# Whole-batch DMA transposes of queries and zero-padded keys in an attention and convolution kernel on one core

## The chip, the cores and the metric

One core of one Trainium2 chip. The metric is device time in microseconds (us) of one execution; medians of several executions are quoted. The kernel before takes 475.0 us (median of 3 runs, 474.39 to 475.42).

## The reference, cut to what matters

```python
B, H, S, D = 8, 12, 448, 64
scores = q @ k.transpose(0, 1, 3, 2) / sqrt(64)          # per batch and head, 448 x 448
attn   = exp(scores - m) / (sum(exp(scores - m)) + exp(-m))
x      = (attn @ v) -> (8, 448, 768)
proj   = x @ w_proj                                       # 768 -> 3 x 768
x1, x2, x3 = thirds of proj
y      = x1 * irfft(rfft(x2) * rfft(filter)) * x3         # along the 448 positions
out    = y @ w_out
```

## The kernel before

The kernel's matmuls contract over the partitions, so queries and keys must lie with the 64 head dimensions on partitions, while memory has positions there. The kernel works in pairs of heads (6 per batch, 48 in all). GpSimd's DMA queue loads a batch with the cast from float32 to bfloat16, and TensorE turns each pair: four key blocks and four query blocks, copied from PSUM by VectorE into a zero-padded key tile and a query tile.

```python
def transposes(A, hp):                       # one unit per pair, cut
    for t in range(4):                       # keys
        nc.tensor.transpose(tb[:, t*128:(t+1)*128], A["kn"][:, hp, t, :], ident_bf)
    for st in range(NST):                    # queries
        nc.tensor.transpose(tb[:, 512 + ...], A["qf"][:, st, hs, :], ident_bf[:SP, :SP])
    nc.vector.tensor_copy(z[0:64, 4:0:-1, :], tk[0:64])
    nc.vector.tensor_copy(z[64:128, 4:8, :], tk[64:128])
    nc.vector.tensor_copy(qT, tq)

# order of one pair's units ("cur" is scored, "old" is summed, "nxt" is turned)
sc(0); sc(1); av(0); T(nxt); sc(2); av(1); sc(3); back(old); folds(old)
```

Between these units the main loop puts dense units (projection, spectrum, gate, output) of the batch before, in a fixed ratio of listed costs. Each engine runs its instructions in program order: in the changed kernel below, TensorE does nothing for 44 us behind one waiting matmul. Batch 0 is loaded as float32 by SyncE's queue and cast by the engines.

The softmax here doesn't subtract the row's maximum and nothing guards it: scores larger than these inputs give would overflow.

## Time and profile before

| | before |
|---|---|
| time | 475.0 us |
| busy: TensorE, VectorE, ScalarE | 426.3, 307.3, 288.2 us of a span of 472.9 |
| TensorE busy from 200 to 250 us | 49.03 of 50 |
| one batch in steady state | 52.6 us |
| TensorE full from | 65.6 us |
| tail after TensorE's last attention unit (it starts at 429.63 us) | about 43 us, on TensorE dense work alone |

The prediction shows the main lines. VectorE's copies behind the transposes, from the groups by shape (line, engine, operation, out<-in, count | busy us, mean ns | idle before):

```profile
L338 DVE COPY kz<-tps 64x512 bf16<-64x512 bf16 x48 | 20.5, 428 | 0.7
L337 DVE COPY kz<-tps 64x512 bf16<-64x512 bf16 x48 | 19.7, 411 | 10.7 <-PE tps L329 10.7
L345 DVE COPY qT<-tps 128x448 bf16<-128x448 bf16 x42 | 16.4, 391 | 0.6
```

And what TensorE waits for from 66 to 420 us (who <- for whom: total us, times, longest), which is nearly nothing and lies in the spectrum units:

```profile
PE xsp L492 <- DVE g L519: 3.2, 7, 0.5
PE xsp L492 <- ACT x L517: 1.7, 7, 0.2
```

### The profile page before, as it was taken

Reading aid. Unit: us, or ns where it says so; the run is one execution under the profiler, and the core shown is the slowest. Engines: PE = TensorE matmul, PEld = TensorE weight load, DVE = VectorE, ACT = ScalarE, POOL = GpSimd, SP = SyncE. Lnnn points to the kernel's source line nnn. Section 1 sums busy time; section 2 is a strip of 40 time slices with the busy share of each in tenths; the row PEclk is TensorE's granted clock in tenths of the full one; section 3 lists DMA queues with packets and bytes.
Section 4 is the critical chain, followed back from the end, with each engine's and each line's share of the span. In section 5 each row is a group of like instructions: output and inputs, shape, how many; then the busy total and the mean of one; then the engine's idle time right before and its main releaser. Section 6 shows DMA issues by size and latency. Waiting matters only on the chain.

```text
span 472.9 us, 9624 instructions
## 1 busy us (share of the span) xinstructions
PE 426.3 (90%) x3872; PEld 298.9 (63%) x3872; DVE 307.3 (65%) x892; ACT 288.2 (61%) x493; POOL 109.4 (23%) x146
## 2 busy tenths in 40 slices
PE   0276889999999999999999999999999999999995
PEld 0144457577766777577766777577766777567664
DVE  7778555785569665774579575874578565873450
ACT  1364557666675667566675657657676668563543
POOL 5816391061202610071103510081000000000000
PEclk9998889999999999999999999999999999999999
DMA  7999999099901993097902991096900110003003
GB/s 208 181 231 176 146 161 62 1 73 134 89 1 11 138 129 19 1 88 120 89 1 20 144 129 5 1 101 126 69 1 1 60 60 0 2 2 119 0 1 116
DMA packets 128492, 35.62 MB, mean 75 GB/s; under 512 B 116925, under 2 KB 124864, under 8 KB 128448
## 3 DMA queue, kind: packets, MB, share of 16 engines
q0 software_dynamic: 118080, 19.87, 55.8%
q1 hardware_dynamic: 10368, 15.14, 10.9%
q8 instruction: 30, 0.49, 0.4%
q14 instruction: 14, 0.11, 0.1%
HBM read 43.86 MB, written 11.01 MB: 116 GB/s over the span
## 4 chain that ended last, share of the span: by engine, by line
PE 67%; DVE 14%; ACT 7%; DMA 7%; POOL 3%; issue 1%; SPq 1%; ACTq 0%; DVEq 0%; POOLq 0%
PE pps L508 18%; PE pps L473 10%; PE ops L580 10%; PE sc L353 9%; PE op L372 5%; DMA wproj_bf<-in_moe_w_proj_dram 4%; PE ops L558 3%; ACT xs L493 3%; PE cps L532 2%; PE xsp L492 2%; DVE t L496 2%; PE xps L395 2%; DVE g L519 2%; PE op L367 2%; DVE t L497 2%; ACT e L355 2%
## 5 line engine op out<-in xcount | busy, mean ns | idle before, releaser
L355 ACT ACTIVATE e<-sc 128x896 bf16<-128x896 f32 x144 | 132.6, 922 | 46.7 <-PE sc L353 46.7
L508 PE MATMUL pps<-xT,wproj_bf 128*128 128x448 bf16 x576 | 124.3, 352 | 0.5 <-ACT x L517 0.3
L508 PEld LDWEIGHTS <-wproj_bf 128*128 128x128 bf16 x576 | 53.5, 97 | 44.4 <-issue 3.0
L353 PE MATMUL sc<-qT,kz 128*128 128x448 bf16 x288 | 81.0, 364 | 0.5 <-ACT e L355 0.4
L473 PE MATMUL pps<-wproj_bf,xf 128*113 128x384 bf16 x384 | 72.2, 326 | 0.5 <-ACT x L480 0.5
L372 PE MATMUL op<-vn,e 128*128 128x65 bf16 x1152 | 58.1, 195 | 0.0
L473 PEld LDWEIGHTS <-xf 128*113 128x113 bf16 x384 | 48.9, 132 | 13.1 <-issue 0.9
L372 PEld LDWEIGHTS <-e 128*128 128x128 bf16 x1152 | 51.4, 98 | 6.8 <-issue 0.7
L580 PE MATMUL ops<-wout_bf,yT 128*112 128x384 bf16 x288 | 53.8, 327 | 0.5 <-ACT osb L568 0.5
L115 POOL DMA_DIRECT2D qf<-in_q_dram x28 | 26.2, 943 | 120.8 <-PE tps L329 84.1
L380 DVE TENSOR_SCALAR rec<-op 128x4 f32<-128x4 f32 x96 | 15.1, 158 | 56.9 <-PE op L372 56.7
L480 ACT CAST x<-pps 113x384 bf16<-113x384 f32 x64 | 30.8, 481 | 34.1 <-PE pps L473 33.8
L517 ACT CAST x<-pps 128x448 bf16<-128x448 f32 x48 | 25.5, 532 | 28.9 <-PE pps L508 26.5
L367 PE MATMUL op<-vr,er 128*128 128x130 bf16 x192 | 42.5, 221 | 0.5
L382 DVE TENSOR_TENSOR xb<-op,rec 128x256 bf16<-128x256 f32 x96 | 40.7, 424 | 3.3
L580 PEld LDWEIGHTS <-yT 128*112 128x112 bf16 x288 | 35.8, 130 | 10.1 <-issue 0.6
L327 PE MATMUL tps<-ident_bf,kn 128*128 128x128 bf16 x192 | 19.5, 224 | 22.1 <-DVE kn L164 18.9
L496 DVE TENSOR_TENSOR t<-xs,hrs 113x768 bf16<-113x768 bf16 (+1 forms) x32 | 17.8, 556 | 32.6 <-ACT xs L493 32.6
L587 ACT COPY osb<-ops 112x384 f32<-112x384 f32 x48 | 23.0, 480 | 23.9 <-PE ops L580 21.3
L353 PEld LDWEIGHTS <-kz 128*128 128x128 bf16 x288 | 27.3, 100 | 15.7 <-issue 3.1
L539 ACT CAST cw<-cps 128x448 bf16<-128x448 f32 x48 | 25.8, 539 | 18.3 <-PE cps L532 18.3
L398 DVE COPY xT<-xps 128x448 bf16<-128x448 bf16 x48 | 18.7, 389 | 26.5 <-PE xps L395 26.5
(97 smaller groups left out, 634.9 us busy)
## 6 DMA issues: line engine op xcount, KB each, us to landing
out_dram<-osb SPq DMA_DIRECT2D x32, 336.0 KB, 2.7
qf<-in_q_dram POOLq DMA_DIRECT2D x28, 168.0 KB, 5.4
vn<-in_v_dram POOLq DMA_DIRECT2D x7, 672.0 KB, 10.1
kn<-in_k_dram POOLq DMA_DIRECT2D x42, 96.0 KB, 4.7
wproj_bf<-in_moe_w_proj_dram POOLq DMA_DIRECT2D x3, 1152.0 KB, 14.0
sq<-in_q_dram SPq DMA_DIRECT2D x6, 224.0 KB, 6.5
sk<-in_k_dram SPq DMA_DIRECT2D x6, 192.0 KB, 6.4
sv<-in_v_dram SPq DMA_DIRECT2D x6, 192.0 KB, 4.6
```

The lines of the kernel that those rows point to most:

```text
L115: nc.gpsimd.dma_start(A["qf"][:, st, :, :], q[b, :, st * SP : (st + 1) * SP, :].rearrange("h p d -> p h d"),)
L353: nc.tensor.matmul(sc[:, u, 0:S], P["z"][:, (4 - t, 4 + t)[u], :], P["qT"])
L355: nc.scalar.activation(e, sc[:, :, 0:S], AF.Exp, scale=SCALE)
L367: nc.tensor.matmul(op[:, i, :, :], e[0][:, qs], A["vr"][:, hp, :, :], start=True, stop=False)
L372: nc.tensor.matmul(op[:, i, u, :], e[1 + t][:, u, qs], A["vn"][:, hp, 4 * u + t, :], start=False, stop=(u == 1 and t == 2),)
L382: nc.vector.tensor_tensor(A["xb"][:, 2 * hf : 2 * hf + 2, 2 * hp : 2 * hp + 2, :], op[:, :, :, 0:DH], rec[:].unsqueeze(3).to_broadcast([12 ...
L473: nc.tensor.matmul(pps[:FQ, :DCH], xf[:, pg, kt, 0:FQ], wproj_bf[:, kt, D + ch * DCH : D + (ch + 1) * DCH], start=(kt == 0), stop=(kt == N ...
L480: nc.scalar.copy(T["x2"][:, pg, ch * DCH : (ch + 1) * DCH], pps[:FQ, :DCH])
L496: nc.vector.tensor_tensor(t1[:K], xs[:K], hrs[:K, par, :, cs], op=ALU.mult)
L508: nc.tensor.matmul(p[:, :S], wproj_bf[:, kt, 2 * part * D + dt * 128 : 2 * part * D + (dt + 1) * 128], xT[:, kt, 0:S], start=(kt == 0), st ...
L539: nc.scalar.copy(cw[:, dt % 2, :, :], cps[:, 0:S].rearrange("p (a n) -> p a n", a=2))
L580: nc.tensor.matmul(ops_[:SP, :DCH], yT[:, dt, st * SP : (st + 1) * SP], wout_bf[:, dt, ch * DCH : (ch + 1) * DCH], start=(dt == 0), stop=( ...
```

## The change

Its intent is to take the 42 transpose units of batches 1 to 7 off TensorE and their copies off VectorE. The loads go into one tile `nat`, keys already zero-padded, and SyncE's queue turns it by DMA into two alternating whole-batch key tiles `kz` and query tiles `qT`. `nat` also serves as the float32 staging area of batch 0, so the load of batch 1 moves behind batch 0's casts. To let it go first, two projection parts, the filter and the output weights are issued after it, and the first dense units are put in the order in which their weights arrive. Cut to its core:

```diff
-    kn = [const.tile([128, NHP, 4, 128], BF16, ...) for i in range(2)]
-    kz = [const.tile([128, 8, 128], BF16, ...) for i in range(3)]
+    kz = [const.tile([128, NHP, 7, 128], BF16, ...) for i in range(2)]
+    nat = const.tile([128, NHP * 7 * 128 + NST * D], BF16, name="nat")
+    kp, qn = (views of nat: padded keys, queries)
...
+    def turn(A):
+        for st in range(NST):
+            nc.sync.dma_start(A["qT"][:, :, st*SP:(st+1)*SP], qn[:, st] ..., transpose=True)
+        nc.sync.dma_start(A["kz"] ..., kp ..., transpose=True)
...
-            if nxt:
+            if nxt and nxt[0] == 0:
                 units.append(T(nxt))
...
-        U = [G(0, 0), G(0, 1)] + ...                     # dense units
+        if b == 0:                                       # in order of the weights
+            U = [all P] + [G(0..1)] + [filter_spectrum] + [Z and G(2..3) in turns]
...
-    RATIO = 1.9
+    RATIO = 2.2
...
-                if b == 0 and hp == 2:
-                    wproj_load(0); wproj_load(2)
                 if b == 0 and hp == 4:
-                    F = filter_load(); state[1] = attn_load(1); wout_load()
+                    memset(the padding of kp)
+                    state[1] = attn_load(1)
+                    wproj_load(0); wproj_load(2)
+                    state["F"] = filter_load(); wout_load()
+                if hp == (5 if b == 0 else 3) and b + 1 < n_batches:
+                    turn(state[b + 1])
```

More of the change, by code (lines that the diff above doesn't have):

```diff
@@ L80 @@
     hrs = wts.tile([FQ, 2, 2, D], BF16, name="hrs")
-    kn = [const.tile([128, NHP, 4, 128], BF16, name=f"kn{i}") for i in range(2)]
+    kz = [const.tile([128, NHP, 7, 128], BF16, name=f"kz{i}") for i in range(2)]
+    nat = const.tile([128, NHP * 7 * 128 + NST * D], BF16, name="nat")
+    kp = nat[:, 0 : NHP * 7 * 128].rearrange("p (g t c) -> p g t c", g=NHP, t=7)
+    qn = nat[0:SP, NHP * 7 * 128 :].rearrange("p (t h d) -> p t h d", t=NST, h=H)
+    ks = const.tile([128, NHP, 128], BF16, name="ks")
     vn = [const.tile([128, NHP, 7, DH + 1], BF16, name=f"vn{i}") for i in range(2)]
     vr = [const.tile([128, NHP, 2, DH + 1], BF16, name=f"vr{i}") for i in range(2)]
-    kz = [const.tile([128, 8, 128], BF16, name=f"kz{i}") for i in range(3)]
     def constants(i):
-        nc.gpsimd.memset(kn[i][:, :, 0, :], 0.0)
+        if i == 0:
+            nc.gpsimd.memset(ks, 0.0)
         nc.gpsimd.memset(vr[i], 0.0)
@@ L98, in batch_tiles @@
     def batch_tiles(b):
-        A = {"b": b, "kn": kn[b % 2], "vn": vn[b % 2], "vr": vr[b % 2]}
-        A["qf"] = ld.tile([SP, NST, H, DH], BF16, name="qf")
+        A = {"b": b, "vn": vn[b % 2], "vr": vr[b % 2], "kz": kz[b % 2]}
+        A["qT"] = qtp.tile([128, NHP, S], BF16, name="qT")
         A["xb"] = xbp.tile([128, NST, H, DH], BF16, name="xb")
-        A["xT"] = xtp.tile([128, NDT, S + 2], BF16, name="xT")
+        A["xT"] = xtp.tile([128, NDT, S + 2], BF16, name="xT", tag="xT")
         A["xf"] = fold.tile([128, 4, NDT, FQ + 1], BF16, name="xf", tag="xf")
@@ L115, in attn_load @@
             nc.gpsimd.dma_start(
-                A["qf"][:, st, :, :],
+                qn[:, st, :, :],
                 q[b, :, st * SP : (st + 1) * SP, :].rearrange("h p d -> p h d"),
@@ L121, in attn_load @@
             for t in range(3):
-                nc.gpsimd.dma_start(A["kn"][:, :, 1 + t, c], kr[:, :, 4 * u + t, :])
-            nc.gpsimd.dma_start(A["kn"][c, :, 0, c], kr[c, :, 3, :])
+                nc.gpsimd.dma_start(kp[:, :, (2 - t, 4 + t)[u], c], kr[:, :, 4 * u + t, :])
+            nc.gpsimd.dma_start(kp[c, :, 3, c], kr[c, :, 3, :])
         nc.gpsimd.dma_start(
@@ L128, in attn_load, with staged_load, stage @@
         return A
-    def staged_load(b, sp, tp):
+    def turn(A):
+        for st in range(NST):
+            nc.sync.dma_start(
+                A["qT"][:, :, st * SP : (st + 1) * SP],
+                qn[:, st, :, :].rearrange("p h d -> p (h d)"),
+                transpose=True,
+            )
+        nc.sync.dma_start(
+            A["kz"][:].rearrange("p g t c -> p (g t) c"),
+            kp[:].rearrange("p g t c -> p (g t c)"),
+            transpose=True,
+        )
+    def staged_load(b):
+        both = xtp.tile([128, 2, NHP, DH], F32, name="rests", tag="xT")
         A = batch_tiles(b)
         A["staged"] = True
+        nf = nat.bitcast(F32)
+        def stage(hp, at, n):
+            o = (hp % 3) * 1280 + at
+            return nf[:, o : o + n]
         def rows(x, hp):
@@ L142, in shared, with load @@
             return bass.AP(x.tensor, o, [[DH, 128], [2 * S * DH, NHP], [1, DH]])
-        for hp in range(NHP):
+        def load(hp):
             for name, x in (("k", k), ("q", q), ("v", v)):
                 if name == "q":
-                    t = A["sq", hp] = sp.tile([SP, 2, NST, DH], F32, name="sq")
+                    t = A["sq", hp] = stage(hp, 768, 512)[0:SP].rearrange(
+                        "p (u j d) -> p u j d", u=2, j=NST
+                    )
                     nc.sync.dma_start(
-                        t[:].rearrange("p u j d -> p u (j d)"),
+                        t.rearrange("p u j d -> p u (j d)"),
                         q[b, 2 * hp : 2 * hp + 2].rearrange("u (p j) d -> p u (j d)", j=NST),
@@ L152, in staged_load @@
                     continue
-                t = A[f"s{name}", hp] = sp.tile([128, 2, 3, DH], F32, name=f"s{name}")
-                nc.sync.dma_start(t[:].rearrange("p u j d -> p u (j d)"), rows(x, hp))
+                t = A[f"s{name}", hp] = stage(hp, 384 * "kv".index(name), 384).rearrange(
+                    "p (u j d) -> p u j d", u=2, j=3
+                )
+                nc.sync.dma_start(t.rearrange("p u j d -> p u (j d)"), rows(x, hp))
                 if hp == 0:
-                    R = A[f"s{name}r"] = tp.tile([128, NHP, DH], F32, name=f"s{name}r")
+                    R = A[f"s{name}r"] = both[:, "kv".index(name)]
                     nc.sync.dma_start(R, shared(x))
+        A["load"] = load
+        for hp in range(3):
+            load(hp)
         return A
@@ L163, in cast_shared @@
             if name == "k":
-                eng.tensor_copy(A["kn"][c, :, 0, c], A["skr"][c])
+                eng.tensor_copy(ks[c, :, c], A["skr"][c])
             else:
@@ L168, in cast_k @@
     def cast_k(A, hp, eng):
-        eng.tensor_copy(
-            A["kn"][:, hp, 1:4, :].rearrange("p j (u d) -> p u j d", u=2), A["sk", hp]
-        )
+        t = A["kn", hp] = ld.tile([128, 3, 128], BF16, name="kn")
+        eng.tensor_copy(t[:].rearrange("p j (u d) -> p u j d", u=2), A["sk", hp])
     def cast_q(A, hp, eng):
-        dst = A["qf"][:, :, 2 * hp : 2 * hp + 2, :].rearrange("p j u d -> p u j d")
+        t = A["qn", hp] = ld.tile([SP, NST, 2, DH], BF16, name="q0")
+        dst = t[:].rearrange("p j u d -> p u j d")
         if eng is nc.scalar:
@@ L182, in cast_v @@
             eng.tensor_copy(A["vn"][:, hp, 4 * u : 4 * u + 3, 0:DH], A["sv", hp][:, u])
+        if hp + 3 < NHP:
+            A["load"](hp + 3)
     def tables(tp):
@@ L324, in transposes @@
         tb = tps.bitcast(BF16)
-        hs = slice(2 * hp, 2 * hp + 2)
-        for t in range(4):
-            nc.tensor.transpose(tb[:, t * 128 : (t + 1) * 128], A["kn"][:, hp, t, :], ident_bf)
+        nc.tensor.transpose(tb[:, 0:128], ks[:, hp, :], ident_bf)
+        for t in range(1, 4):
+            nc.tensor.transpose(
+                tb[:, t * 128 : (t + 1) * 128], A["kn", hp][:, t - 1, :], ident_bf
+            )
         for st in range(NST):
             nc.tensor.transpose(
-                tb[:, 512 + st * SP : 512 + (st + 1) * SP], A["qf"][:, st, hs, :], ident_bf[:SP, :SP]
+                tb[:, 512 + st * SP : 512 + (st + 1) * SP], A["qn", hp][:, st, :, :], ident_bf[:SP, :SP]
             )
-        qT = qtp.tile([128, S], BF16, name="qT")
-        z = kz[(A["b"] * NHP + hp) % 3]
+        z = A["kz"][:, hp]
         tk = tb[:, 0:512].rearrange("p (t c) -> p t c", t=4)
-        nc.vector.tensor_copy(z[0:64, 4:0:-1, :], tk[0:64])
-        nc.vector.tensor_copy(z[64:128, 4:8, :], tk[64:128])
+        nc.vector.tensor_copy(z[0:64, 3::-1, :], tk[0:64])
+        nc.vector.tensor_copy(z[64:128, 3:7, :], tk[64:128])
         tq = tb[:, 512 : 512 + S]
-        if "staged" in A:
-            nc.vector.tensor_copy(
-                qT[:].rearrange("p (c j) -> p j c", j=NST), tq.rearrange("p (j c) -> p j c", j=NST)
-            )
-        else:
-            nc.vector.tensor_copy(qT, tq)
-        A[hp] = {"qT": qT, "z": z, "e": []}
+        nc.vector.tensor_copy(
+            A["qT"][:, hp, :].rearrange("p (c j) -> p j c", j=NST),
+            tq.rearrange("p (j c) -> p j c", j=NST),
+        )
     def scores(A, hp, t):
-        P = A[hp]
+        P = A.setdefault(hp, {"e": []})
         sc = psc.tile([128, 2, 512], F32, name="sc")
@@ L352, in scores @@
             for u in range(2):
-                nc.tensor.matmul(sc[:, u, 0:S], P["z"][:, (4 - t, 4 + t)[u], :], P["qT"])
+                nc.tensor.matmul(sc[:, u, 0:S], A["kz"][:, hp, (3 - t, 3 + t)[u], :], A["qT"][:, hp, :])
             e = etp.tile([128, 2, S], BF16, name="e")
@@ L356, in scores @@
         else:
-            nc.tensor.matmul(sc[:, 0, 0:S], P["z"][:, 4, :], P["qT"])
+            nc.tensor.matmul(sc[:, 0, 0:S], A["kz"][:, hp, 3, :], A["qT"][:, hp, :])
             e = erp.tile([128, S], BF16, name="er")
@@ L601, in V, with first @@
             return (0.38, lambda: inverse(dt))
-        U = [G(0, 0), G(0, 1)]
-        U += [P(pg, ch) for pg in range(2) for ch in range(2)]
-        U += [P(2, 0), Z(0, 0), P(2, 1), P(3, 0), Z(0, 1), P(3, 1)]
-        U += [G(1, 0), Z(1, 0), G(1, 1), G(2, 0), Z(1, 1), G(2, 1), G(3, 0), G(3, 1)]
+        def first():
+            U = [G(0, 0), G(0, 1)]
+            U += [P(pg, ch) for pg in range(2) for ch in range(2)]
+            U += [P(2, 0), Z(0, 0), P(2, 1), P(3, 0), Z(0, 1), P(3, 1)]
+            U += [G(1, 0), Z(1, 0), G(1, 1), G(2, 0), Z(1, 1), G(2, 1), G(3, 0), G(3, 1)]
+            return U
+        if b == 0:
+            U = [P(pg, ch) for pg in range(4) for ch in range(2)]
+            U += [G(0, 0), G(0, 1), G(1, 0), G(1, 1), (2.6, lambda: filter_spectrum(state["F"]))]
+            gs = [G(2, 0), G(2, 1), G(3, 0), G(3, 1)]
+            for i in range(4):
+                U += [Z(*divmod(i, 2)), gs[i]]
+        else:
+            U = first()
         U += [V(0), G(4, 0), V(1), G(4, 1), V(2), G(5, 0), V(3), V(4), G(5, 1), V(5)]
@@ L618 @@
         tc.tile_pool(name="tabs", bufs=1) as tp,
-        tc.tile_pool(name="stage", bufs=3) as sp,
-        tc.manual_schedule(engines={E.PE, E.Pool, E.DVE, E.Activation}),
+        tc.manual_schedule(engines={E.PE, E.Pool, E.DVE, E.Activation, E.SP}),
     ):
-        state = {0: staged_load(0, sp, tp)}
+        state = {0: staged_load(0)}
         make_identity(nc, ident_bf)
         constants(0)
-        for z in kz:
-            nc.vector.memset(z, 0.0)
+        nc.vector.memset(kz[0][64:128, :, 0:3, :], 0.0)
+        nc.vector.memset(kz[0][0:64, :, 4:7, :], 0.0)
         tables(tp)
@@ L644 @@
                     constants(1)
-                if b == 0 and hp == 2:
+                if b == 0 and hp == 4:
+                    nc.vector.memset(kp[:, :, 0:3, 64:128], 0.0)
+                    nc.vector.memset(kp[:, :, 4:7, 0:64], 0.0)
+                    for u in range(2):
+                        nc.vector.memset(
+                            kp[64 * u : 64 * u + 64, :, 3, 64 - 64 * u : 128 - 64 * u], 0.0
+                        )
+                    state[1] = attn_load(1)
                     wproj_load(0)
                     wproj_load(2)
-                if b == 0 and hp == 4:
-                    F = filter_load()
-                    state[1] = attn_load(1)
+                    state["F"] = filter_load()
                     wout_load()
@@ L656 @@
             emit()
-            if what == "X" and hp == NHP - 1:
-                if b == 0:
-                    filter_spectrum(F)
+            if hp == NHP - 1 and (what, part) == (("X", 0) if b else ("F", 2)):
                 queue += dense(state[b])
```

## The prediction

> **What bounds the kernel now.** I read the page's busy line and its forty slices first, then the timeline of TensorE over one batch, then GpSimd's and SyncE's timelines, then the groups by shape, and the first 66 us last. Busy time and slices, from the page:
>
> ```profile
> PE 426.3 (90%) x3872; PEld 298.9 (63%) x3872; DVE 307.3 (65%) x892; ACT 288.2 (61%) x493; POOL 109.4 (23%) x146
> ...
> PE   0276889999999999999999999999999999999995
> ...
> DVE  7778555785569665774579575874578565873450
> ACT  1364557666675667566675657657676668563543
> ...
> DMA  7999999099901993097902991096900110003003
> ```
>
> From the seventh slice (a slice is 11.8 us) to the last but one, TensorE is full and no other engine is; in the first five it is not. So there are two stages with two limits: a steady stretch in which only TensorE work counts, and a start in which something else does. The stretch table (busy us with counts, clock, DMA share, GB/s) confirms it:
>
> ```profile
> 40.00:60.00 20.00, 13.61 (x143) 8.92 (x144) 13.92 (x44) 10.50 (x13) 12.19 (x14) 0.83 1.93 152
> ...
> 200.00:250.00 50.00, 49.03 (x468) 35.30 (x467) 32.86 (x98) 32.84 (x57) 13.03 (x15) 1.00 0.77 70
> ```
>
> In steady state TensorE has 1 us idle in 50 at full clock. The chain of waits shows the same piece (L558, first output rows) at 106.52, 159.14, 211.75 and 264.36: a period of 52.6 us a batch. What a transpose unit costs there, from TensorE's timeline (start, us, instructions):
>
> ```profile
> 202.71 0.39 PE L327 MATMUL tps<-ident_bf,kn 128*128 128x128 bf16 x4
> 202.94 0.36 PE L329 MATMUL tps<-ident_bf,qf 112*128 112x112 bf16 x4
> 203.13 0.55 PE L532 MATMUL cps<-bt,yh 113*128 113x224 bf16 x4
> ```
>
> The duration of one (219 ns in the groups) is not its cost, since they overlap. The start of the next work less the start of the unit is: 203.13 - 202.71 = 0.42 us for eight transposes. Units at 220.17, 227.38 and 236.55 give 0.43, 0.42, 0.42.
>
> The start: scores of batch 1 begin at 55.04 us, the pair after them at 65.57, and from there TensorE is full (dense matmuls from 65.76). Before 44 us, one pair of batch 0 takes 4.9 us (scores of its first tile at 31.77, 36.67, 41.56), VectorE having hardly a gap: copies, casts and a 1.15 us query copy.
>
> **What the Trainium skill says.** (1) "DMA: Bandwidth & Descriptors", section "Latency and other measured facts", gives a DMA transpose 261 GB/s with a non-contiguous middle dimension, about 350 to 400 when contiguous. The kernel before has none, so its trace can't agree or disagree. (2) The same page, "Queues, rings and completion order": a DMA engine takes turns between the queues that have work, packet by packet. So a transpose beside a casting load should get about half. (3) "VectorE: DVE Perf Modes", section "The three transpose paths", has 390 ns for a 128x128 on TensorE and 1309 ns on DMA. The trace contradicts the first as a cost in a stream: 0.42 us for eight, 53 ns each. The second, if it were the cost of each block, would be fatal (rivals).
>
> **The change part by part.**
> Removed: the transpose units of batches 1 to 7, 7 x 6 = 42. TensorE: 42 x 0.425 = 17.9 us; all but the first one or two lie after 65.57, where TensorE is the limit: 40.5 x 0.425 = 17.2 us off the end. VectorE: 42 x (0.409 + 0.428 + 0.391) = 51.6 us from the groups of kz and qT copies, on an engine that is two thirds busy, so worth only the short waits that VectorE causes TensorE: 0.24 and 0.46 us per period near 247 us. I credit 2 us over the run. The ratio of dense to attention units goes from 1.9 to 2.2 because a pair's listed cost falls from 2.94 to 2.52: 17.64 x 1.9 = 33.5 and 15.12 x 2.2 = 33.3, against 32.7 of dense units. The interleaving and the tail stay as they were.
>
> Added: per batch 4 x 112 x 768 x 2 B = 0.69 MB of queries and 128 x 5376 x 2 B = 1.38 MB of padded keys, turned by SyncE's queue. At 261 GB/s that is 2.6 and 5.3 us of transfer.
>
> In steady state this must fit into the period. One tile takes the loads, so loads and turns alternate. GpSimd's timeline:
>
> ```profile
> 203.60 3.73 POOL L115 DMA_DIRECT2D qf<-in_q_dram  x4 [21.97 <-PE tps L329]
> 207.31 2.48 POOL L122 DMA_DIRECT2D kn<-in_k_dram  x3
> ...
> 212.85 0.73 POOL L123 DMA_DIRECT2D kn<-in_k_dram  x1
> 223.14 2.04 POOL L124 DMA_DIRECT2D vn<-in_v_dram  x1 [9.56 <-issue]
> ```
>
> Queries and keys take from 203.6 to about 217 (last issue 212.85, landing 3.8 to 4.5 later): 13 us. With 10 to 16 us of turning the cycle is 23 to 29 us of a period of 50. It should hide, with 20 us to spare. SyncE's other work, four output writes from 215.35 to 224.5, precedes a turn and doesn't fill the period either.
>
> Moved, and here it costs: the load of batch 1 now waits for the staged buffers, which share its memory, until the casts of the last pair of batch 0, on VectorE at 44.44 and 44.71 us:
>
> ```profile
> 44.44 0.35 DVE L169 CAST kn<-sk 128x384 bf16<-128x384 f32 x1
> 44.71 0.42 DVE L178 CAST qf<-sq 112x512 bf16<-112x512 f32 x1
> ```
>
> The memsets of the padding follow (1152 elements twice, 384 twice; at the 485 ns of 512 32-bit words of the old memset, 1.5 us), but only the keys wait for them, after 3.7 us of query issues. I add 0.5 us for the larger memset at the beginning. So the load starts at 45.7, its keys have landed 13 us later at 59, and the whole-batch key transpose can't start before. It moves 5.3 us alone; beside the values and weights that follow on the other queue, twice that at worst; with some 2 us from issue to landing (the output writes take 2.7) 7.3 to 12.6 us. I take 10.5. Scores of batch 1 start at 69.5 us instead of 55.04. TensorE executes in order, and dense work of batch 0 is emitted behind these scores, so it waits, from about 52.
>
> From there: the first pair of batch 1 with its folds, about 6 us (before, 55.04 to 59.9 for the pair and 2 us of folds). Then the same work as before 65.57 to 472.9, which is 407.3, less 17.2, less 2. To this comes the filter's spectrum, done before 65.57 until now: 16 matmuls in 2.6 us at full clock, but eight ScalarE copies of 0.48 behind three buffers, so about 4. Sum: 69.5 + 6 + 407.3 - 17.2 - 2 + 4 = 467.6; the timed runs are 2 us longer than the profile's span (475.0 against 472.9). **469.6 us.**
>
> The weights' new order: the second projection part is issued at 13 us as before. The other two, 1.18 MB each, and the filter follow the load; at the 0.15 MB/us of the casting loads (2.06 MB of a batch in 9.3 + 4.6 us of transfer) they land near 72, 80 and 85 us, some 5 later beside transposes. Dense units in their new order want them at about 87 and 94 (69.5 + 6, then eight units of 0.97 us with attention between: 11 us). No wait there. Batch 2's keys land near 101 and are turned by 114; its scores want them at 69.5 + 50 = 120. This is the tightest place in the run.
>
> **The rivals.** (a) The start costs nothing: the key transpose runs at 350 GB/s and is favoured, 6 us; scores at 65, total 465, a gain of 2.1%. For it: the skill's rate for contiguous blocks. Against: values and weights fill the DMA in just these microseconds (DMA share 1.93 from 40 to 60). (b) The transposes are slow. At the 1309 ns of a lone block, 42 key blocks and 24 of queries make over 80 us a batch: more than the period, the cycle of one tile becomes the bound, and seven times 95 us give over 700. A milder form, 25 us for the keys, gives scores at 84, a late batch 2, and 485 to 490. Against: a lone block's time is mostly latency. (c) ScalarE becomes the bound in steady state: 32.84 of 50 us becomes 32.84 of 47.5, 69%. Unlikely. (d) The saving on VectorE is the gain: its share was no limit, so this would add nothing beyond the 2 us. (e) VectorE's memsets are dearer than I think, 16-bit at half the rate: 2 us more.
>
> **Range and chances.** The steady gain of 17 to 19 us is nearly sure if the turns hide; the start takes back 10 to 18. The main uncertainty is the rate of a transpose, which nothing in this trace measures, and its tail is on the slow side. 462 is a turn of 6 us with everything else in favour by 3; 485 is a turn of 25. Under 465.5 (2%) I need the keys turned in some 6.5 us: one in three. Over 484.5, one in eight.
>
> **What would show it right or wrong.** Right: the period falls from 52.6 to 50.0 to 50.2 us; TensorE idles from about 52 to 69.5 us, waiting for the DMA of kz; after that it is full; VectorE's busy time falls by some 50 us. Wrong: a wait for kz or qT at the start of batches 3 to 7 (cycle of the tile), a period over 51, or key transposes that take much less or more than 10.5 us from issue to landing.

## More of the kernel before

`av(0)` and `av(1)`, the halves of the weighted sum, share one PSUM buffer, which VectorE empties (`rec`, `xb`).

## The result and the profile after

The changed kernel takes 504.9 us (median of 4 runs, 504.0 to 505.35), with the kernel before at 474.7 in the same rounds: a ratio of 1.0637, interval 1.0608 to 1.0666. A ratio here is the mean time of one kernel's fast runs over that of the other's of the same rounds, so it is not quite the ratio of the medians quoted.

The busy line and slices of the page after (a slice is now 12.6 us):

```profile
PE 408.3 (81%) x3536; PEld 279.6 (56%) x3536; DVE 260.8 (52%) x769; ACT 285.3 (57%) x493; POOL 109.0 (22%) x145
...
PE   0365300199899998999999899999999999999995
...
DMA  6825999999809994599649973996293020003003
```

TensorE's busy time fell by 18.0 us (17.9 forecast) and VectorE's by 46.5 (51.6 forecast). But TensorE is empty in the sixth and seventh slice, while the DMA is full there. TensorE's timeline has one line for it (start, us, what, and in brackets the idle time before and who ended it), and SyncE's queue names the transfer:

```profile
99.27 0.56 PE L391 MATMUL sc<-qT,kz 128*128 128x448 bf16 x1 [44.29 <-DMA kz<-nat]
...
48.73 7.74 SPq L140 DMA_TRANSPOSE qT<-nat  x4
63.35 30.07 SPq L145 DMA_TRANSPOSE kz<-nat  x1
...
373.39 6.95 SPq L145 DMA_TRANSPOSE kz<-nat  x1
```

The key transpose of batch 1 was issued at 63.35 and landed 35.9 us later, at 99.2. The last one, of batch 7, issued when nearly nothing else was loaded, took 8.8 us. The table by stretches shows both stages; columns are the stretch, its length, busy us with counts of TensorE, its weight loads, VectorE, ScalarE and GpSimd, then clock, DMA share and GB/s:

```profile
60.00:80.00 20.00, 0.00 (x0) 0.00 (x0) 0.00 (x0) 0.00 (x0) 5.11 (x9) 0.50 1.73 184
...
200.00:250.00 50.00, 48.22 (x430) 33.50 (x428) 28.02 (x87) 33.58 (x60) 13.04 (x15) 1.00 1.06 112
```

In steady state the same dense piece (first output rows) starts at 150.75 us and, six batches on, at 453.10: a period of 50.39 us in place of 52.61. VectorE has 28 us of work in 50 in place of 33. But TensorE is idle a little more than before, not less (1.8 us in 50 against 1.0), and the waits from 106 to 450 us have new names:

```profile
PE op L401 <- DVE xb L416: 5.1, 9, 1.0
PE xps L429 <- DVE xb L416: 1.9, 4, 0.8
PE hps L341 <- DVE uw L333: 1.5, 1, 1.5
```

What the 35.9 us were spent on is told by the DMA view. From 68 to 92 us, by queue (packets, MB, share of the 16 engines): q0 is GpSimd's, with the weights, q1 is SyncE's, with the transpose.

```profile
q0 software_dynamic: 2988, 3.98, 93.2%
q1 hardware_dynamic: 2972, 0.76, 24.3%
```

The packets are equal in number to half a per cent, the bytes are not: a weight packet is 3.98 MB / 2988 = 1.3 KB on average (1536 bytes for a row of 768 bfloat16), a packet of the transpose 0.76 MB / 2972 = 256 bytes. In this stretch the transpose got 16% of the bytes. The queues keep step in time too: counted in order in the kept trace from 68.5 to 92 us, the lead of one over the other stays within 14 packets, less than one for each of the 16 engines. Groups of packets, taken in turn, would hardly keep so close.

After the weights, the queries of batch 2 follow on q0 in packets of 128 bytes, and the same transpose goes faster. From 92 to 99 us:

```profile
q0 software_dynamic: 3812, 0.48, 106.0%
q1 hardware_dynamic: 2436, 0.62, 67.0%
```

So the 35.9 us are 4.75 before the first packet of the transpose, 23.9 for 2972 packets beside the weights, 6.4 for the other 2436 beside short packets, and 0.9 to the landing.

### The profile page after: what moved, and what is told of

It is laid out like the page before. It is cut to its first block, busy times and chain, and to the rows that moved or that the text cites. A ratio compares the mean times of both kernels' runs of the same rounds, so it can differ in the third digit from the quotient of the medians.

```text
span 503.5 us, 8928 instructions
## 1 busy us (share of the span) xinstructions
PE 408.3 (81%) x3536; PEld 279.6 (56%) x3536; DVE 260.8 (52%) x769; ACT 285.3 (57%) x493; POOL 109.0 (22%) x145
## 2 busy tenths in 40 slices
DMA packets 186057, 50.02 MB, mean 99 GB/s; under 512 B 174493, under 2 KB 182432, under 8 KB 186016
## 4 chain that ended last, share of the span: by engine, by line
PE 62%; DVE 15%; DMA 9%; ACT 7%; issue 4%; POOL 2%; POOLq 0%; SPq 0%; ACTq 0%; DVEq 0%
PE pps L542 15%; PE pps L507 11%; PE ops L614 9%; PE sc L387 7%; DMA kz<-nat 7%; PE op L406 6%; PE cps L566 3%; PE ops L592 3%; ACT e L389 2%; PE op L401 2%; ACT xs L527 2%; DMA nat<-in_k_dram 2%; PE xps L429 2%; PE sc L391 1%; DVE xb L416 1%
## 5 line engine op out<-in xcount | busy, mean ns | idle before, releaser
L387 PE MATMUL sc<-qT,kz 128*128 128x448 bf16 x288 | 81.1, 365 | 0.3 <-ACT e L389 0.3
L507 PE MATMUL pps<-wproj_bf,xf 128*113 128x384 bf16 x384 | 72.3, 327 | 1.1 <-DVE xf L447 0.5
L393 ACT ACTIVATE er<-sc 128x448 bf16<-128x448 f32 x48 | 26.3, 547 | 57.4 <-PE sc L391 57.3
L507 PEld LDWEIGHTS <-xf 128*113 128x113 bf16 x384 | 48.8, 132 | 14.5 <-issue 1.1
L391 PE MATMUL sc<-qT,kz 128*128 128x448 bf16 x48 | 17.5, 366 | 47.2 <-DMA kz<-nat 44.3
L129 POOL DMA_DIRECT2D nat<-in_k_dram x42 | 34.8, 851 | 55.8 <-DMA kz<-nat 55.8
L131 POOL DMA_DIRECT2D vn<-in_v_dram x7 | 14.3, 2039 | 98.6 <-issue 98.6
```

Of the source, the lines that this page charges most:

```text
L129: nc.gpsimd.dma_start(kp[:, :, (2 - t, 4 + t)[u], c], kr[:, :, 4 * u + t, :])
L387: nc.tensor.matmul(sc[:, u, 0:S], A["kz"][:, hp, (3 - t, 3 + t)[u], :], A["qT"][:, hp, :])
L393: nc.scalar.activation(e, sc[:, 0, 0:S], AF.Exp, scale=SCALE)
L507: nc.tensor.matmul(pps[:FQ, :DCH], xf[:, pg, kt, 0:FQ], wproj_bf[:, kt, D + ch * DCH : D + (ch + 1) * DCH], start=(kt == 0), stop=(kt == N ...
```

## The experiments

Theory A: the DMA engines take turns between the two queues, one packet each, and the loss is the long weight packets beside the transpose. Theory F, for the smaller part: the transpose unit was also a filler between `av(0)` and `av(1)`. The rivals stand in the expectations. Eight kernels ran, all with correct results. Two drafts failed to build before (a DMA with four dimensions; batch 1's extra tiles didn't fit the memory until they shared tiles used later).

### e1: the late weights behind the transpose

```diff
                     state[1] = attn_load(1)
-                    wproj_load(0); wproj_load(2); state["F"] = filter_load(); wout_load()
...
                     turn(state[b + 1])
+                    if b == 0:
+                        rest(state[1])
+                        nc.gpsimd.tensor_copy(gate, state[1]["kz"][:, 5, 6, 0:8])   # waits for the transpose
+                        wproj_load(0); wproj_load(2); state["F"] = filter_load(); wout_load()
```

> The two late projection parts, the filter and the output weights are issued only when batch 1's key transpose has landed (a small GpSimd copy reads its result first). Theory A (turn-taking by packet: a 256-byte packet of the transpose for each 1536-byte packet of the weights): the key transpose of batch 1, issued near 63 us, lands after 10 to 13 us in place of 35.9, with only the values of batch 1 beside it; batch 1's scores start near 75 in place of 99.3; the total is 480 to 486 us, less than the full 24 us better because batch 2's load now comes behind the weights. Rival B (the first whole-batch transpose is slow of itself, whatever runs beside it, as its 30 us on SyncE's queue could suggest): it still takes over 30 us, and the late weights make the total 505 or more.

483.7 us, ratio 1.019 (1.016 to 1.0219). The DMA view from 62 to 76 us gives the transpose with its time from issue to landing, and TensorE starts batch 1 at 71.96 (10 to 13 us and a start near 75 were expected):

```profile
kz<-nat SPq DMA_TRANSPOSE x1, 9.2
...
71.96 0.56 PE L393 MATMUL sc<-qT,kz 128*128 128x448 bf16 x1 [18.42 <-DMA kz<-nat]
...
125.56 0.36 PE L393 MATMUL sc<-qT,kz 128*128 128x448 bf16 x1 [3.06 <-DMA kz<-nat]
```

The first whole-batch transpose is not slow of itself: rival B falls. It moves at 290 GB/s here once values and weights are out of the way; before that, 2.8 of its 9.2 us pass without a packet of it, while 2901 packets of 128 bytes go on the other queue. As expected, batch 2 comes late: 3.06 us of waiting at 125.56.

### e2 and e8: the same bytes in shorter packets

```diff
-        nc.gpsimd.dma_start(wproj_bf[:, :, cs], moe_w_proj[:, cs]...)
+        for e in range(12):                        # e8: range(3), pieces of 256
+            es = slice(part * D + 64 * e, part * D + 64 * e + 64)
+            nc.gpsimd.dma_start(wproj_bf[:, :, es], moe_w_proj[:, es]...)
```

The output weights likewise; the small copy that waits for batch 1's values was put before the filter.

> Same bytes, same order, beside the same transpose, but the two late projection parts and the output weights go in pieces of 64 columns, so that their packets are 128 bytes and not 1536 (the filter stays). Theory A: the transpose gets two thirds of the bytes in place of a seventh, and lands 14 to 17 us after its issue at 63, scores of batch 1 near 79, total 482 to 489 us. Rival C (the transpose yields to whatever bytes the other queue holds, or shares by bytes): 30 us or more from issue to landing as in the changed kernel, total 500 to 507.

490.9 us, ratio 1.034 (1.0295 to 1.0384), over the 482 to 489 expected. The transpose lands 19.7 us after its issue, not 35.9: the direction is theory A's, though my 14 to 17 was too low. The DMA view from 70 to 80 us:

```profile
q1 hardware_dynamic: 4148, 1.06, 79.9%
q0 software_dynamic: 4150, 0.52, 79.3%
```

One for one again, and now two thirds of the bytes go to the transpose. What I had left out is the beginning: in the first 5.05 us after the issue (4.75 in the changed kernel) no packet of the transpose moves, while first the batch's values drain in 128-byte packets and then some weights go. 5408 packets at 415 pairs a microsecond are 13 us, and 5 before them make 18 of the 19.7.

> As e2_short_packets, but pieces of 256 columns, so packets of 512 bytes. If turns are taken strictly packet for packet, the pair of packets costs between the 38.6 ns of e2 (4150 pairs in 10 us on 16 engines) and the 129 ns of the changed kernel (2988 pairs in 24 us), about 63 ns by interpolation over the size: 5400 packets in 21 us plus some 3 for the filter's long packets and 4 to 5 before the first byte, so the key transpose of batch 1 lands 26 to 30 us after its issue, between the 19.7 of e2 and the 35.9 of the changed kernel; the counts of packets of the two queues agree within 3% in a stretch where both run; total 496 to 500 us. If the sharing has nothing to do with the packet's size and e2 gained by something else in its order (the smaller copy behind the values, many small issues), it lands within 22 us and the total is near 491.

499.5 us, ratio 1.0526 (1.0504 to 1.0548). The transpose lands 30.1 us after its issue, just over the 26 to 30 expected, and between 68 and 84 us the packets of the two queues agree to one in a thousand:

```profile
q0 software_dynamic: 3864, 1.94, 87.6%
q1 hardware_dynamic: 3862, 0.99, 46.5%
...
kz<-nat SPq DMA_TRANSPOSE x1, 30.1
```

So the time of the same transpose is set by the size of the packets beside it: 35.9 us beside 1536 bytes (for 2972 of its 5408 packets; the rest went beside short ones), 30.1 beside mostly 512, 19.7 beside 128, 9.2 with none behind the values. Rival C, which yields to bytes, falls.

### e3: the weights early, in the old places

```diff
+                if b == 0 and hp == 2:
+                    wproj_load(0); wproj_load(2)
                 if b == 0 and hp == 4:
+                    state["F"] = filter_load()
                     memset(the padding of kp)
                     state[1] = attn_load(1)
-                    wproj_load(0); wproj_load(2); state["F"] = filter_load(); wout_load()
...
+                    (output weights behind the transpose, as in e1)
```

> Weights in the old places (projection parts 0 and 2 at the third pair, the filter before batch 1's load), where the changed kernel leaves the DMA idle from 28 to 45 us; the output weights behind the transpose. The new order of the first dense units stays. Theory A: transposes only beside batch 1's own values, 10 to 13 us, scores of batch 1 near 75, no late batch 2, total 478 to 483 us: about 24 of the 30 us lost go back, and what stays over 475 is the wait for load and turn. Rival B: the transpose takes over 30 us all the same, total 503 or more.

477.75 us, ratio 1.0073 (1.0046 to 1.01), just better than expected. The key transpose takes 9.4 us and batch 1's scores start at 72.3. Moving the weights out of the idle DMA stretch (28 to 45 us) into the transpose's way cost 504.9 - 477.75 = 27 us. It also shows that the change without this part still doesn't beat the kernel before: TensorE waits from 53 to 72 us for a batch that must be loaded and turned whole.

### e4: batch 1 turned on TensorE

```diff
+    B1[0] = (keys of batch 1, in the memory of a dense tile used later)
+    B1[1] = (queries of batch 1, in the memory of the output tiles)
+    nc.gpsimd.memset(kz[1] padding, 0.0)
...
-            if nxt and nxt[0] == 0:  T(nxt)
+            if nxt and nxt[0] == 0:  T(nxt)
+            T(1, 0), T(1, 1) at the last pair of batch 0; T(1, 2), T(1, 3) in the next; T(1, 4), T(1, 5) behind its folds
...
     (loads of weights and batch 1, first dense units: as in the kernel before; DMA transposes from batch 2)
```

> Batch 1 is loaded into tiles of its own in the old way, at the old time, and turned on TensorE (two units each at the last pair of batch 0 and in the first pair of batch 1, the last two behind the folds); DMA transposes only from batch 2; weights and first dense units in the old order. If the loss is all in the wait for batch 1, TensorE never waits for a kz transpose, dense work starts near 66 to 70 us as in the kernel before, the period is 50.4 us, and the total is 459 to 466 us, faster than both kernels. If DMA transposes cost something in steady state too (rival D), the period stays over 51 and the total over 468.

463.9 us, ratio 0.9783 (0.9758 to 0.9808): faster than both. No wait for a tile turned by DMA is left, and the period is 50.02 us (162.71 to 412.80 in five batches), with six whole-batch turns per run that cost nothing on the path. Rival D falls: in steady state the DMA transposes are hidden. The edit also puts weights, filter and first dense units back in their old order, so it doesn't weigh these parts singly.

### e5 and e6: one score unit moved

```diff
             sc(0)
-            sc(1)
             av(0)
+            sc(1)
```

e5 does this to the changed kernel, e6 to e4.

> The changed kernel with one line moved: the first half of a pair's weighted sum stands before the second score unit instead of behind it, so two score units and not one lie between the two halves. Theory F (the transpose unit was also a filler: without it TensorE comes to the second half before VectorE has emptied the one buffer of the first, 5.1 us in 9 waits from 106 to 450 us, 1.9 us more for the transposes back): most of these waits go, the period falls from 50.4 to 49.6 to 50.0 us and the total from 504.9 to 499 to 502. Rival G (what is missing of the steady gain is ScalarE's exponentials or the DMA, or TensorE simply falls into the next wait): 503.5 to 506.

> The same move on the kernel with batch 1 turned on TensorE (463.9 us). Theory F: its 8.3 us of waits for the second half (14 waits) shrink to 3 or less, period 49.3 to 49.7 in place of 50.0, total 458 to 461. Rival G: 463 to 465.

e5: 501.6 us, ratio 1.0602 (1.057 to 1.0633). e6: 460.2 us, ratio 0.9728 (0.9696 to 0.9761). By the medians that is 3.2 and 3.7 us; by the ratios, which take out the drift of the kernel before between the two jobs, 0.35 and 0.55 points, 1.7 and 2.6 us, with intervals that still overlap. The profiles are clearer than the times. In e5 the wait for the second half falls from 5.1 to 1.1 us (106 to 450 us), while that of the transposes back rises from 1.9 to 3.5, and the period goes from 50.39 to 49.92 us (148.87 to 448.39 in six batches). For e4 and e6, TensorE's waits that the view lists from 106 to 420 us, first e4:

```profile
PE op L416 <- DVE xb L431: 5.8, 12, 0.9
```

and e6, all of them:

```profile
PE xps L444 <- DVE xb L431: 2.0, 6, 0.3
PE ops L612 <- DVE yT L601: 1.8, 7, 0.3
PE xsp L546 <- DVE xT L447: 0.2, 1, 0.2
```

The wait for the second half is gone, 4.0 us of others stand where 5.8 were, and the period fell from 50.02 to 49.45 us (160.66 to 407.90). Theory F holds, but rival G has a share: part of what is won falls into the next wait, more so in e5. How such a wait comes about can be read in the changed kernel's timeline at 177 us:

```profile
177.66 0.56 DVE L530 TENSOR_TENSOR t<-xs,hrs 113x768 bf16<-113x768 bf16 x1 [2.48 <-ACT xs L527]
...
179.14 0.15 DVE L414 TENSOR_SCALAR rec<-op 128x4 f32<-128x4 f32 x1
179.33 0.18 DVE L415 RECIPROCAL rec<-rec 128x4 f32<-128x4 f32 x1
179.54 0.42 DVE L416 TENSOR_TENSOR xb<-op,rec 128x256 bf16<-128x256 f32 x1
...
180.02 0.23 PE L401 MATMUL op<-vr,er 128*128 128x130 bf16 x1 [0.72 <-DVE xb L416]
```

VectorE is idle for 2.48 us, waiting for ScalarE with a spectrum unit's products at the head of its queue; only behind these does it empty the weighted sum, which TensorE had finished by 177.5, and TensorE stands for 0.72 us. VectorE's lower load doesn't help here, since its order is the limit.

### e7: the zeros of e6 written by ScalarE

```diff
-            nc.gpsimd.memset(kz[1][64:128, :, 0:3, :], 0.0)
-            nc.gpsimd.memset(kz[1][0:64, :, 4:7, :], 0.0)
...
+        nc.scalar.copy(kz[1][64:128, :, 0:3, :], kz[0][64:128, :, 0:3, :])
+        nc.scalar.copy(kz[1][0:64, :, 4:7, :], kz[0][0:64, :, 4:7, :])
```

> The kernel of e6_best_order; the zeros in batch 1's key tile are written by ScalarE, idle until 10.5 us, and no longer by GpSimd between 15 and 20 us, where VectorE's small table instructions took up to 1.99 us in place of 0.34 and TensorE's first transposes waited for 22.0 us in place of 17.2 to 19.0. If the GpSimd memsets slowed VectorE there: first transposes at 17 to 19 us, total 456 to 459 (460.2 before it). If not: 459 to 462.

457.2 us, ratio 0.9638 (0.9613 to 0.9663), the best: 3.6% faster than the kernel before, and 0.9 points better than e6 with intervals that lie apart. The suspicion came from the start of e4, VectorE and GpSimd:

```profile
15.85 1.99 DVE L316 TENSOR_SCALAR bt<-sn,inv 113x224 bf16<-113x224 f32 x1 [1.02 <-ACT sn L272]
17.76 2.40 DVE L319 TENSOR_SCALAR bt<-sn 113x672 bf16<-113x672 f32 x1
...
15.69 2.01 POOL L103 MEMSET kz<- 64x2304 bf16 x1
17.76 2.03 POOL L104 MEMSET kz<- 64x2304 bf16 x1
```

The two VectorE instructions end just behind the two GpSimd memsets, by 0.14 and 0.37 us. In e7 they are short:

```profile
15.73 0.85 DVE L314 TENSOR_SCALAR bt<-sn,inv 113x224 bf16<-113x224 f32 x1 [1.02 <-ACT sn L270]
16.49 0.51 DVE L317 TENSOR_SCALAR bt<-sn 113x672 bf16<-113x672 f32 x1
```

The first transposes on TensorE wait until 18.0 us in place of 22.0. That the memsets slowed VectorE is shown. The Trainium skill tells in "SBUF — State Buffer", section "SBUF: two separate sides", of an exclusive lock on the ports that VectorE and GpSimd share; the ends in e4 agree with it, but no run tells it from another way of sharing.

## Why the prediction was wrong

It said 469.6 us with a range of 462 to 485; 504.9 lies outside. By its own steps:

- **TensorE's saving.** Right. 0.425 us a unit, 2.55 us a batch, gave a period of 50.06; measured 50.39, with 18.0 us less busy time in all. e6, with the filler put right, reaches 49.45.
- **Does the turning fit into a period?** Right. Key turns in the later batches take 12.8 to 14.5 us, the last one 8.8, and there is no wait for `kz` or `qT` after the first.
- **The start of batch 1's load.** Right: 45.7 predicted, 44.79 measured.
- **The landing of its keys.** Off by 4.3 us. I let the last keys land 3.8 to 4.5 us after their issue, as before the change. They took 9.0, and the key transpose was issued at 63.35, not at 59. Since 48.7 us the query transposes ran beside these loads, which I had not put into the sum. That they are the cause is argued, not tested.
- **The key transpose: the step that failed.** "Beside the values and weights that follow on the other queue, twice that at worst." It was 35.9 us against 10.5, and these 25.4 us with the 4.3 make up, but for rounding, the 29.8 by which TensorE's start was late (99.3 against 69.5). I had read in the skill that turns are taken packet by packet and then wrote "about half", which is half of the packets. I never asked how long a packet is. The row lengths were in the code (768 elements for a weight row, 64 for a key row), and the page before even counted packets by size. e1, e2, e8 and e3 show the rule: one packet each, so 256 bytes of the transpose for each 1536 of weights. The sum also lacked the 4.75 us before the first packet, whose cause is open. The rate of a transpose alone, my stated main uncertainty, was near enough (261 GB/s assumed, 290 in e1).
- **From the start of batch 1 to the end.** 398.1 us predicted (467.6 - 69.5), 404.2 measured (503.5 - 99.3): 6.1 us too few. I credited 2 us for waits on VectorE that would vanish. They did (the spectrum's waits of 3.2 and 1.7 us are 0.2 each in the changed kernel), but waits for the weighted sum took their place. Removing an instruction group from a busy engine also removed what covered the latency of another. e5 and e6 give back 1.7 to 3.7 us of this; how the rest divides, between the filter's spectrum (1.5 us of wait) and the like, was not tested.
- **The rivals.** The mild form of (b), a slow turn, came closest in effect, "25 us for the keys", but I gave it a slow transpose as its cause. No rival named the neighbour's packets. With one in eight for slower by over 2%, I weighed this side too lightly. In its severe form, seven times 95 us are 665 us, and over 700 only with the start.

The sum closes: 29.8 + 6.1 = 35.9 us of span, less 0.6 because the median of 504.9 lies 1.4 us above the profiled span and not 2.0, is 35.3, the difference of 504.9 and 469.6.

The intended gain is real: 10 us once batch 1 is kept off this path (e4: 463.9 against 474.15 in the same rounds), 13 with the filler put right (e6: 460.2 against 472.9). The changed kernel loses this three to four times over in one wait of 44.3 us at the start.

## What to carry to other kernels

Before two DMA streams are put side by side, compare the sizes of their packets, not their bytes: a stream of short packets beside one of long packets got only its packet's share here, and a latency-critical transfer belongs before or behind bulk weights, or the weights into idle DMA time or shorter rows. When a whole-batch transform replaces a piecewise one, look for the first batch: its full latency stood on the path here, and only from the second on was it hidden. And before taking a unit out of a full engine's order, ask what it was covering.

## What the Trainium skill lacked or had wrong

- "DMA: Bandwidth & Descriptors", "Queues, rings and completion order": turns by packet are confirmed, but the page calls a packet a group of some 9 to 17 descriptors. Between these two queues the turns were one record of the trace each, 256 bytes against 128, 512 or 1536: 4148 to 4150, 3862 to 3864, 2972 to 2988. Whether such a record is a packet or a descriptor in the page's sense, no run shows. The page doesn't say what follows for the shares: the same transpose took 19.7, 30.1 and 35.9 us.
- The same page, "Latency and other measured facts", has 261 GB/s for transposes with a non-contiguous middle dimension, about 350 to 400 contiguous. A key transpose of 1.38 MB in 42 blocks ran at 290 GB/s once it moved, between the two, and took 8.8 to 9.4 us from issue to landing with little beside it.
- No page: a transpose issued while short casting packets drain moved no packet for the first 2.8 to 5.1 us (e1 2.8, e3 3.1, the changed kernel 4.75, e8 4.8, e2 5.05). Its cause is open.
- "VectorE: DVE Perf Modes", "The three transpose paths": 1309 ns for a 128x128 block by DMA is no cost per block in a large transfer. 42 blocks in 9.2 us (e1) are 0.22 us each. Nor is 390 ns on TensorE the cost of one in a stream: eight took 0.42 us.
